# Batch 1's k.v as corner products, later exponentials and earlier output copies at the first seam of a fused attention and SwiGLU kernel

## The chip, the cores and the metric

One core of a Trainium2 chip. The metric is device microseconds of one execution. A run's time is about 1.8 us longer than the span that its profile shows (before: 310.9 against 309.1).

## The reference

Linear attention over 8 batches, 8 heads, 576 positions and head size 64, then a SwiGLU block over 4608 tokens:

```python
phi = lambda x: np.where(x > 0, x, np.exp(x) - 1.0) + 1.0
q_p, k_p = phi(q), phi(k)
kv  = np.einsum('bhsd,bhse->bhde', k_p, v)
z   = np.sum(k_p, axis=2)
num = np.einsum('bhsd,bhde->bhse', q_p, kv)
den = np.einsum('bhsd,bhd->bhs', q_p, z)[..., None] + 1e-06
x   = (num / den)            # brought to 4608 x 512
g   = x @ w_gate             # 512 x 1536
out = (g / (1 + np.exp(-g)) * (x @ w_val)) @ w_out
```

## The kernel before

The tokens go through in nine groups (0 to 8) of 512. For each group TensorE does a first product (twelve blocks of gate and value, `l1`) and a second product (`l2`, four output blocks for groups 0 and 1). The attention of later batches is woven between these blocks as lists of functions, one list for each block. On each engine the order of the program is the order of execution. The seam from group 0 to group 1 is the part that the change touches:

```python
    # batch 1's k.v: 64 rows by 128 columns, of which only two 64x64 corners are wanted
                    if b < 2:
                        nc.tensor.matmul(
                            out=kvb[b][hh][:, 256 * lp:256 * lp + P], lhsT=term_[rows, j, P * lp:P * lp + P],
                            rhs=v16[b][rows, 2 * lp:2 * lp + 2, D * j:D * j + D], ...)
                        continue
                    for e in range(2):                      # batch 2 and later: the corners alone
                        nc.tensor.matmul(
                            out=kvb[b][hh][D * e:D * e + D, 256 * lp:256 * lp + D + 1], ...)
    # ... cut ...
    def phi(src, e, dst, b, lp):          # batch 2: VectorE, min, then max and add fused
        s = slice(2 * lp, 2 * lp + 2)
        nc.vector.tensor_scalar(out=e[:, s, :], in0=e[:, s, :], scalar1=1.0, scalar2=None, op0=ALU.min)
        for l in range(2 * lp, 2 * lp + 2):
            nc.vector.scalar_tensor_tensor(out=dst[...], in0=src[...], scalar=0.0, in1=e[...], op0=ALU.max, op1=ALU.add)
    # ... cut ...
        w = at(12, [     # (after which of group 0's twelve output pieces, what)
            (0, lambda: t1(pX[0], 0, 4, A)), (1, lambda: t1(pX[1], 4, 7, V)), (1, lambda: z0(1, 0)),
            (1, lambda: z0(1, 1)), (1, lambda: z0_copy(1, 0)), (1, lambda: z0_copy(1, 1)),
            (2, lambda: t1(pX[0], 7, 9, A)), (2, lambda: mm1(1, 0)), (2, lambda: mm1(1, 1)), (2, lambda: r1_copies()),
            (3, lambda: den1(0)), (4, lambda: num1(0)), (4, lambda: exp_k(2, 0)), (5, lambda: den1(1)),
            (5, lambda: phi_k(2, 0)), (6, lambda: num1(1)), (6, lambda: exp_k(2, 1)), (7, lambda: den2()),
            (9, lambda: phi_k(2, 1)), (10, lambda: num2()), (10, lambda: exp_q(2, 0)), (11, lambda: exp_q(2, 1))])
    # ... cut ...
    for i in range(3):
        # ... cut ...
        for t in range(4):
            l2(0, t, 4 * i, 4 * i + 4)         # one piece: 4 matmuls of 128x512
            for f in w[4 * i + t]:
                f()
            if i == 2:
                l2_out(0, t, V)                # VectorE copies the bank out, SyncE stores it
```

`den1` and `num1` are products of 64x64 corners (denominators and numerators of batch 1; their operands `zz` and `R` are VectorE's copies of batch 1's k sums and k.v), `den2` and `num2` their tail of two columns of units; in the old `num2` VectorE's four tail products follow at once. A stretch of such 64x64 products between two 128-row blocks is called a visit below. `t1` is a transpose by TensorE, `mm1` is k.v, `exp_k`, `exp_q` and `l1_gate`'s silu run on ScalarE. `joint(2)` in group 1 needs batch 2's k sums and v copies; its `zd` and `R` copies lead to batch 2's normalising.

The last group's results leave in 16 store issues of 64 KB, 13 of them on SyncE's queue, two on ScalarE's and one on GpSimd's.

Of the kernel before, what the change touches and what calls it, by code (L numbers as in the profile page):

```python
# [13 lines left out]
P = 128  # L14
# [3 lines left out]
def kernel(  # L18
# [81 lines left out]
    def ld_k(b):  # L100
        load(k, k16, b)
# [11 lines left out]
    def ld_w2(i):  # L113
        nc.gpsimd.dma_start(out=wo[:, 4 * i:4 * i + 4, :],
                            in_=moe_w_out[512 * i:512 * i + 512, :].rearrange("(c p) f -> p c f", p=P))
# [3 lines left out]
        s = slice(2 * lp, 2 * lp + 2)  # L119
        nc.scalar.activation(out=e[:, s, :], in_=src[b % 2][:, s, :], func=AF.Exp, bias=0.0, scale=1.0)  # L120

    def phi(src, e, dst, b, lp):
        s = slice(2 * lp, 2 * lp + 2)
        nc.vector.tensor_scalar(out=e[:, s, :], in0=e[:, s, :], scalar1=1.0, scalar2=None, op0=ALU.min)
        for l in range(2 * lp, 2 * lp + 2):
            nc.vector.scalar_tensor_tensor(
                out=dst[b % 2][:, :, D * l:D * l + D],
                in0=src[b % 2][:, l, :].rearrange("p (j d) -> p j d", d=D), scalar=0.0,
                in1=e[:, l, :].rearrange("p (j d) -> p j d", d=D), op0=ALU.max, op1=ALU.add)

    def relu(src, dst, b, lp):
        s = slice(2 * lp, 2 * lp + 2)
        nc.scalar.activation(out=dst[b % 2][:, :, P * lp:P * lp + P].rearrange("p j (s d) -> p s j d", d=D),
# [9 lines left out]
    def phi_sum(e, dst, b, lp):  # L143
        s = slice(2 * lp, 2 * lp + 2)
        nc.vector.tensor_scalar(out=e[:, s, :], in0=e[:, s, :], scalar1=1.0, scalar2=None, op0=ALU.min)
        d = dst[b % 2][:, :, P * lp:P * lp + P].rearrange("p j (s d) -> p s j d", d=D)
        nc.vector.tensor_tensor(out=d, in0=d, in1=e[:, s, :].rearrange("p s (j d) -> p s j d", d=D), op=ALU.add)

    def exp_k(b, lp):
        exp_(k16, ek, b, lp)  # L150

    def exp_q(b, lp):
        exp_(q16, eq, b, lp)

    def phi_k(b, lp):
        phi_sum(ek, kp, b, lp) if b > 2 else phi(k16, ek, kp, b, lp)

    def phi_q(b, lp):
        phi_sum(eq, qp, b, lp) if b > 2 else phi(q16, eq, qp, b, lp)


    def vcast(b, lp):
# [12 lines left out]
    def mm1(b, lp):  # L175
        if lp == 0:
            kvb[b] = ((pV[2], pX[0]), (pX[2], pV[2]), (pX[0], pX[1]), (pV[0], pG[0]), (pX[2], pV[2]))[min(b, 4)]
        for j in range(J):
            for (t, term_) in enumerate(terms_k(b, lp)):
                for hh in range(2):  # L180
                    rows = slice(C * hh, C * hh + C)
                    if b < 2:
                        nc.tensor.matmul(
                            out=kvb[b][hh][:, 256 * lp:256 * lp + P], lhsT=term_[rows, j, P * lp:P * lp + P],
                            rhs=v16[b][rows, 2 * lp:2 * lp + 2, D * j:D * j + D],
                            start=(j == 0 and t == 0), stop=(j == J - 1 and t == len(terms_k(b, lp)) - 1))
                        continue
                    for e in range(2):
                        nc.tensor.matmul(  # L189
                            out=kvb[b][hh][D * e:D * e + D, 256 * lp:256 * lp + D + 1],  # L190
                            lhsT=term_[rows, j, P * lp + D * e:P * lp + D * e + D],
                            rhs=vm[b % 2][rows, j, 2 * lp + e, :], start=(j == 0), stop=(j == J - 1))

    def zdiag(b, lp):
        for hh in range(2):
# [9 lines left out]
                                 bias=0.0, scale=1.0)  # L205

    def kv(b):
        c1 = D if b < 2 else 0
        return lambda i, e: R[b % 2][D * e:D * e + D, i, c1 * e:c1 * e + D]

    def zs(i, e):
# [53 lines left out]
    def corners(ps, lhs, b, j0, j1, lps=(0, 1)):  # L265

        for lp in lps:
            for hh in range(2):
                for e in range(2):
                    rows = slice(D * e, D * e + D)  # L270
                    nc.tensor.matmul(out=ps[2 * lp + e][C * hh:C * hh + C, :], lhsT=lhs(2 * lp + hh, e),  # L271
                                     rhs=qT[b % 2][rows, j0:j1, lp, C * hh:C * hh + C], start=True, stop=True)
# [455 lines left out]
    ld_w2(0)  # L728
    ld_v(1)
    ld_w2(1)  # L730
    ld_k(2)
    ld_w2(2)


    def at(n, items):
        sl = [[] for _ in range(n)]
        for (i, f) in items:
            sl[i].append(f)
        return sl
# [8 lines left out]
    def t1(ps, j0, j1, eng):  # L748
        pt = ps[:, :].bitcast(FP16)
        for jj in range(j1 - j0):  # L750
            for lp in range(2):
                i = 2 * jj + lp
                nc.tensor.transpose(out=pt[:, P * i:P * i + P], in_=qp[1][:, j0 + jj, P * lp:P * lp + P],
                                    identity=id16[:, :])
        dst = qT[1][:, j0:j1, :, :].rearrange("p j l t -> p (j l t)")
        if eng == "A":
            nc.scalar.activation(out=dst, in_=pt[:, 0:2 * P * (j1 - j0)], func=AF.Copy, bias=0.0, scale=1.0)
        else:
            nc.vector.tensor_copy(out=dst, in_=pt[:, 0:2 * P * (j1 - j0)])
# [4 lines left out]
    def den1(lp):  # L764
        corners({2 * lp + e: dbank[e][:, 0:W7] for e in range(2)}, zs, 1, 0, 7, (lp,))
        ln0([b[:, 0:W7] for b in dbank], rr[:, 2 * lp:2 * lp + 2, 0:W7])
        exp_neg(rr[:, 2 * lp:2 * lp + 2, 0:W7])
# [12 lines left out]

    def num2():
        corners([nbank[m % 2][:, part1[m]] for m in range(4)], kv(1), 1, 7, 9)
        for m in range(4):
            x0(nbank[m % 2][:, part1[m]], r8[:, m % 2, part1[m]], xT[m][0][:, 0:W2])

    def r1_copies():
        for hh in range(2):
            nc.vector.tensor_copy(out=R[1][:, hh:4:2, 0:P],
                                  in_=kvb[1][hh][:, :].rearrange("p (i c) -> p i c", i=2)[:, :, 0:P])

    def block(src, e, dst):
        for lp in range(2):
            exp_(src, e, 1, lp)
            term(src[1], dst[1], lp, 0.0, ALU.max)
        for lp in range(2):
            phi_1(src, e, dst, lp)

    def first():
        sl = at(FB, [
            (3, lambda: block(k16, ek, kp)), (8, lambda: block(q16, eq, qp)),  # L800
            (11, lambda: nc.scalar.preload_act_table_set("natural_log_exp_and_others"))])
        w = at(12, [
            (0, lambda: t1(pX[0], 0, 4, A)), (1, lambda: t1(pX[1], 4, 7, V)), (1, lambda: z0(1, 0)),
            (1, lambda: z0(1, 1)), (1, lambda: z0_copy(1, 0)), (1, lambda: z0_copy(1, 1)),
            (2, lambda: t1(pX[0], 7, 9, A)), (2, lambda: mm1(1, 0)), (2, lambda: mm1(1, 1)), (2, lambda: r1_copies()),
            (3, lambda: den1(0)), (4, lambda: num1(0)), (4, lambda: exp_k(2, 0)), (5, lambda: den1(1)),
            (5, lambda: phi_k(2, 0)), (6, lambda: num1(1)), (6, lambda: exp_k(2, 1)), (7, lambda: den2()),
            (9, lambda: phi_k(2, 1)), (10, lambda: num2()), (10, lambda: exp_q(2, 0)), (11, lambda: exp_q(2, 1))])
        return sl, w

    def joint(b):
# [7 lines left out]
    def steady(b):  # L819

        n = 5 if b == 2 else 2 if b == 3 else 1
        items = [(n, lambda: zb(b)), (n, lambda: zb_copy(b)), (n, lambda: s3_prod(b, 0)),
                 (n + 1, lambda: s3_reduce(b, 0)), (n + 2, lambda: s3_recip(b, 0)), (n + 2, lambda: s3_prod(b, 1)),
                 (n + 3, lambda: s3_scale(b, 0)), (n + 4, lambda: s3_reduce(b, 1)), (n + 4, lambda: tr(b, 0)),
                 (n + 5, lambda: s3_recip(b, 1)), (n + 5, lambda: s3_prod(b, 2)), (n + 6, lambda: s3_scale(b, 1)),
                 (n + 7, lambda: s3_reduce(b, 2)), (n + 7, lambda: tr(b, 1)), (n + 8, lambda: s3_recip(b, 2)),
                 (n + 9, lambda: s3_scale(b, 2)), (n + 9, lambda: tr(b, 2))]
        if b == 2:
            items = [(0, lambda: vcast(2, 0)), (1, lambda: vcast(2, 1)), (1, lambda: phi_q(2, 0)),
                     (2, lambda: phi_q(2, 1)), (3, lambda: joint(2))] + items  # L830
        elif b == 3:
            items = [(0, lambda: phi_q(b, 1))] + items
        return at(FB, [x for x in items if x[0] < FB]), at(4, [(0, f) for (i, f) in items if i >= FB])
# [48 lines left out]
    for i in range(3):  # L882
        if i < 2:
            for m in range(4):
                w_sum(nc.gpsimd, m, 2 * i, 2 * i + 2)
        for t in range(4):
            l2(0, t, 4 * i, 4 * i + 4)
            for f in w[4 * i + t]:
                f()
            if i == 2:  # L890
                l2_out(0, t, V)
    nc.scalar.preload_act_table_set("silu_and_others")

    for g in range(1, NG):
# [87 lines left out]
```

## Time and profile before

| | before |
|---|---|
| time, median of 4 runs | 310.88 us (310.32 to 311.22) |
| span of the profiled run | 309.12 us |
| TensorE busy | 299.3 us, 97% |
| first group-0 output piece to group 1's third weight block | 18.56 us (38.83 to 57.39) |
| group 1's third weight block to its first output block | 20.17 us (57.39 to 77.56) |
| start of TensorE's last matmul to the end of the span | 6.28 us (302.84 to 309.12) |

The last two rows are differences of start times in the timeline; they leave out the run-to-run scatter of the start (the first group-0 output piece starts anywhere from 38.5 to 39.7 us; what sets it was not followed up).

The page, kernel before: the span, and busy us, share and instructions of each engine.

```profile
span 309.1 us, 6601 instructions
PE 299.3 (97%) x2551; PEld 183.0 (59%) x2551; DVE 252.0 (82%) x536; ACT 217.3 (70%) x336; POOL 48.2 (16%) x62
```

Timeline, kernel before, the seam (start us, duration us, engine, line, operation, out<-in; in brackets idle time before and what ended it):

```profile
53.32 1.43 DVE L126 SCALAR_TENSOR_TENSOR kp<-k,ek 128x576 f16<-128x576 f16 x2
53.72 1.04 PE L457 MATMUL pG<-wo,hT 128*128 128x512 f16 x4
54.66 0.68 DVE L467 TENSOR_SCALAR osb<-pG 128x512 f32<-128x512 f32 x1
...
55.40 1.02 PE L298 MATMUL pG<-xT,wg 128*128 128x512 f16 x4 [0.65 <-DVE osb L467]
...
56.06 0.68 DVE L467 TENSOR_SCALAR osb<-pV 128x512 f32<-128x512 f32 x1
56.26 1.03 PE L298 MATMUL pV<-xT,wv 128*128 128x512 f16 x4
56.66 0.68 DVE L467 TENSOR_SCALAR osb<-pG 128x512 f32<-128x512 f32 x1
57.39 1.02 PE L298 MATMUL pG<-xT,wg 128*128 128x512 f16 x4
```

Group 0's last output piece (53.72) is followed by group 1's first weight block only at 55.40, when VectorE has copied the bank `pG` out; VectorE was late because it did batch 2's k sum (53.32) first. The third weight block waits in the same way for the copy of 56.66.

Timeline of TensorE alone, kernel before, batch 1's k.v:

```profile
43.34 0.23 PE L183 MATMUL pX<-v,kp 64*128 64x128 f16 x1
...
44.45 1.04 PE L457 MATMUL pG<-wo,hT 128*128 128x512 f16 x4
45.41 0.38 PE L271 MATMUL pX<-qT,zz 64*64 64x448 f16 x4
45.73 1.04 PE L457 MATMUL pV<-wo,hT 128*128 128x512 f16 x4
46.70 0.37 PE L271 MATMUL pX<-qT,R 64*64 64x448 f16 x1
```

k.v takes 43.34 to 44.45, 1.11 us. The piece started at 44.45 has 0.86 us to stream (the distance of unbroken pieces).

Timeline, kernel before, group 1's ninth gate block:

```profile
69.64 1.03 PE L298 MATMUL pV<-xT,wv 128*128 128x512 f16 x4
70.01 0.60 ACT L303 ACTIVATE sil<-pG 128x512 f16<-128x512 f32 x1
70.66 1.02 PE L298 MATMUL pG<-xT,wg 128*128 128x512 f16 x4
```

The block of 70.66 could have started at 70.50 (69.64 + 0.86, the distance of unbroken blocks) and waits for the bank that the silu of 70.01 frees.

### The profile page before, as it was taken

The page shows a single profiled execution, that of the slowest core. Times are in us where ns is not written, and L with a number is a line of the kernel's source. Part 1 is how long each engine was busy: PE and PEld are TensorE (multiplying, and loading weights), DVE is VectorE, ACT ScalarE, POOL GpSimd, SP SyncE. Part 2 cuts the span into 40 slices and gives each one's busy share as a digit, 9 for nine tenths or more (in the row PEclk, how much of TensorE's full clock was granted, in tenths as well). Part 3 has the DMA queues.
Part 4 walks back from the last instruction along what each step waited for, and adds up shares of the span by engine and source line. Part 5 has one row for each costly group of instructions (what it writes and reads, how often), then busy time and mean ns, then how long its engine had stood idle before and what let it go on. Part 6 is the DMA issues. An engine that isn't in the chain of part 4 may idle for free.

```text
span 309.1 us, 6601 instructions
## 1 busy us (share of the span) xinstructions
PE 299.3 (97%) x2551; PEld 183.0 (59%) x2551; DVE 252.0 (82%) x536; ACT 217.3 (70%) x336; POOL 48.2 (16%) x62
## 2 busy tenths in 40 slices
PE   7899999999999999999999999999999999999992
PEld 6544453344444477447744774468446888878781
DVE  3757857888967998998899889997999878968971
ACT  3769969859856968696869686968633578448840
POOL 8535286010200002000200000000000004001200
PEclk9999999999999999999999999999999999999999
DMA  7999999998396228921793133122312140042013
GB/s 97 193 200 199 204 207 209 244 228 141 61 244 123 32 46 133 234 55 27 120 234 56 35 70 71 28 51 62 78 25 51 28 111 2 0 95 46 1 44 94
DMA packets 41424, 32.29 MB, mean 104 GB/s; under 512 B 16352, under 2 KB 37280, under 8 KB 41392
## 3 DMA queue, kind: packets, MB, share of 16 engines
q0 software_dynamic: 20672, 18.94, 39.1%
q1 hardware_dynamic: 20560, 12.79, 17.7%
q8 instruction: 20, 0.33, 0.4%
q10 hardware_dynamic: 160, 0.13, 0.2%
q14 instruction: 12, 0.10, 0.1%
HBM read 37.75 MB, written 9.44 MB: 153 GB/s over the span
## 4 chain that ended last, share of the span: by engine, by line
PE 84%; issue 5%; DMA 3%; DVE 3%; POOL 2%; ACT 1%; POOLq 0%
PE pV L298 22%; PE pG L298 22%; PE pX L513 14%; PE pV L513 4%; PE pV L350 4%; PE pG L350 4%; DMA wv<-in_moe_w_val_dram 3%; PE pX L298 3%; PE pG L457 2%; PE pV L457 2%; PE pX L350 1%; PE pV L271 1%; DVE xT L669 1%; PE pX L189 1%; PE pV L418 1%
## 5 line engine op out<-in xcount | busy, mean ns | idle before, releaser
L298 PE MATMUL pV<-xT,wv 128*128 128x512 f16 x324 | 83.5, 379 | 0.1
L298 PE MATMUL pG<-xT,wg 128*128 128x512 f16 x312 | 80.4, 379 | 0.8 <-DVE osb L467 0.6
L303 ACT ACTIVATE sil<-pG 128x512 f16<-128x512 f32 x78 | 45.9, 597 | 28.7 <-PE pG L298 18.0
L304 DVE SCALAR_TENSOR_TENSOR hT<-pV,sil 128x512 f16<-128x512 f32 x81 | 55.1, 687 | 13.0 <-ACT sil L303 6.8
L298 PEld LDWEIGHTS <-wv 128*128 128x128 f16 x336 | 32.7, 98 | 40.1 <-DMA wv<-in_moe_w_val_dram 0.9
L298 PEld LDWEIGHTS <-wg 128*128 128x128 f16 x336 | 32.2, 98 | 39.3 <-issue 1.8
L513 PEld LDWEIGHTS <-hs 128*128 128x128 f16 x336 | 32.4, 98 | 4.7 <-DVE hs L487 0.5
L390 POOL TENSOR_TENSOR hT<-prod,vm 128x512 f16<-128x512 f16 x6 | 6.9, 1156 | 132.0 <-ACT vm L377 132.0
L513 PEld LDWEIGHTS <-hT 128*128 128x128 f16 x252 | 24.3, 98 | 4.1
L513 PE MATMUL pX<-ws,hs 128*128 128x256 f16 x210 | 25.7, 273 | 0.0
L518 ACT ACTIVATE part<-pX 128x256 f32<-128x256 f32 x35 | 12.8, 381 | 13.2 <-PE pX L513 13.1
L95 POOL DMA_DIRECT2D k<-in_k_dram x7 | 5.2, 750 | 80.3 <-ACT part L518 58.8
L487 DVE TENSOR_TENSOR hs<-hT 128x512 f16<-128x512 f16 (+2 forms) x42 | 17.4, 418 | 0.2
L252 DVE TENSOR_TENSOR qp<-qp,rden 128x768 f16<-128x768 f16 x18 | 17.1, 949 | 0.0
L239 DVE TENSOR_REDUCE den<-prod 128x12 f32<-128x768 f16 x18 | 17.0, 943 | 0.0
L120 ACT ACTIVATE ek<-k 128x1152 f16<-128x1152 f16 x14 | 16.0, 1158 | 0.1
L120 ACT ACTIVATE eq<-q 128x1152 f16<-128x1152 f16 x14 | 15.6, 1167 | 0.0
L513 PE MATMUL pX<-wo,hT 128*128 128x256 f16 x126 | 15.2, 273 | 0.0
L457 PEld LDWEIGHTS <-hT 128*128 128x128 f16 x96 | 8.6, 98 | 10.2 <-issue 0.8
L164 ACT ACTIVATE vm<-v 128x1152 f16<-128x1152 f16 x12 | 14.1, 1178 | 0.0
L523 DVE SCALAR_TENSOR_TENSOR osb<-pX,part 128x256 f32<-128x256 f32 x28 | 10.7, 417 | 2.1 <-PE pX L513 1.9
L457 PE MATMUL pG<-wo,hT 128*128 128x512 f16 x48 | 11.7, 380 | 0.0
(185 smaller groups left out, 537.6 us busy)
## 6 DMA issues: line engine op xcount, KB each, us to landing
out_dram<-osb SPq DMA_DIRECT2D x64, 128.0 KB, 4.0
k<-in_k_dram POOLq DMA_DIRECT2D x7, 576.0 KB, 10.8
q<-in_q_dram POOLq DMA_DIRECT2D x7, 576.0 KB, 11.2
v<-in_v_dram POOLq DMA_DIRECT2D x7, 576.0 KB, 13.9
wg<-in_moe_w_gate_dram POOLq DMA_DIRECT2D x6, 256.0 KB, 11.6
wv<-in_moe_w_val_dram POOLq DMA_DIRECT2D x6, 256.0 KB, 12.0
wo<-in_moe_w_out_dram POOLq DMA_DIRECT2D x3, 512.0 KB, 15.8
out_dram<-osb SPq DMA_DIRECT2D x13, 64.0 KB, 2.0
```

The costliest lines, as they stand in the source:

```text
L120: nc.scalar.activation(out=e[:, s, :], in_=src[b % 2][:, s, :], func=AF.Exp, bias=0.0, scale=1.0)
L164: nc.scalar.activation(out=vm[b % 2][:, :, s, 0:D].rearrange("p j l d -> p l j d"), in_=v16[b % 2][:, s, :].rearrange("p l (j d) -> p l j ...
L239: nc.vector.tensor_reduce(out=den[:, HL * j0:HL * j1], in_=prod[:, 0:j1 - j0, :].rearrange("p j (l d) -> p (j l) d", d=D), axis=AX.X, op=A ...
L252: nc.vector.tensor_tensor(out=qv, in0=qv, in1=rden[:, HL * j0:HL * j1].unsqueeze(2).to_broadcast([P, HL * (j1 - j0), D]), op=ALU.mult)
L298: nc.tensor.matmul(out=ps[:, :], lhsT=src[:, i, P * fb:P * fb + P], rhs=xT[i][g % 2][:, :], start=(i == 0), stop=(i == 3))
L303: nc.scalar.activation(out=s[:, :], in_=pg[:, :], func=AF.Silu, bias=0.0, scale=1.0)
L304: nc.vector.scalar_tensor_tensor(out=hT[g % 2][:, fb, :], in0=pv[:, :], scalar=SC, in1=s[:, :], op0=ALU.mult, op1=ALU.mult)
L350: nc.tensor.matmul(out=dst[:, HN * e:HN * e + HN], lhsT=lhs, rhs=rhs, start=(n in (1, 2, 5) and e == 0 and c == 0), stop=(c == 1), skip_gr ...
L457: nc.tensor.matmul(out=pso[(g, t)][:, :], lhsT=hT[g % 2][:, fb, P * t:P * t + P], rhs=wo[:, fb, :], start=(fb == 0), stop=(fb == FB - 1))
L487: (eng or nc.vector).tensor_tensor(out=o, in0=a, in1=b, op=op)
L513: nc.tensor.matmul(out=(z if n in (2, 3, 5) else x)[:, 0:HD], lhsT=left(f), rhs=right(f), start=(f == 0 and n in (1, 2, 5)), stop=(f == HF ...
L518: nc.scalar.activation(out=part[:, 2 * i + tt, :], in_=(x if from_x else z)[:, 0:HD], func=AF.Copy, bias=0.0, scale=1.0 / SC)
```

## The change

Its intent: shorten batch 1's k.v by corner products, let TensorE pass the seam without waiting for VectorE's copies, start the denominators earlier by putting the ln table load behind the first transposed copy, take work off VectorE (a separate max and add in place of the fused form), and make sure the last third of `wo` is there in time.

```diff
-    def phi(src, e, dst, b, lp):        # ... the fused form, gone
     def phi_k(b, lp):
-        phi_sum(ek, kp, b, lp) if b > 2 else phi(k16, ek, kp, b, lp)
+        phi_sum(ek, kp, b, lp)
     # phi_q the same
@@ mm1
-                    if b < 2:
+                    if b == 0:
@@
+                        w = D if b == 1 else D + 1
                         nc.tensor.matmul(
-                            out=kvb[b][hh][D * e:D * e + D, 256 * lp:256 * lp + D + 1],
+                            out=kvb[b][hh][D * e:D * e + D, 256 * lp:256 * lp + w],
@@ loads
     ld_w2(1)
+    ld_w2(2)
     ld_k(2)
-    ld_w2(2)
@@ the lists at the seam
-        w = at(12, [ ... as above ... ])
+        w = at(13, [
+            (0, lambda: t1(pX[0], 0, 4, A)), (0, ln_set), (1, lambda: t1(pX[1], 4, 7, V)), (1, lambda: z0(1, 0)),
+            (1, lambda: z0(1, 1)), (1, lambda: z0_copy(1, 0)), (1, lambda: z0_copy(1, 1)),
+            (2, lambda: den1(0)), (2, lambda: mm1(1, 0)), (2, lambda: mm1(1, 1)), (2, lambda: r1_copies()),
+            (3, lambda: den1(1)), (3, lambda: num1(0)), (5, lambda: t1(pX[0], 7, 9, V)), (5, lambda: num1(1)),
+            (6, lambda: den2()), (6, lambda: exp_k(2, 0)), (6, lambda: exp_k(2, 1)), (7, lambda: max_2(k16, kp, 0)),
+            (7, lambda: max_2(k16, kp, 1)), (8, lambda: num2()), (9, lambda: phi_k(2, 0)), (9, lambda: exp_q(2, 0)),
+            (11, lambda: exp_q(2, 1)), (12, lambda: x2()), (12, lambda: phi_k(2, 1))])
@@ output copies
             l2(0, t, 4 * i, 4 * i + 4)
+            if (i, t) == (2, 1):
+                l2_out(0, 1, V)
             for f in w[4 * i + t]:
                 f()
-            if i == 2:
+            if i == 2 and t != 1:
                 l2_out(0, t, V)
+    for f in w[12]:
+        f()
```

(Cut: the kv and R indices that follow from the corners, `x2`, which is the second half of the old `num2`, and two `max_2` for q at the start of group 1.)

More of the change, by code (lines that the diff above doesn't have):

```diff
@@ L120, in exp_ @@
         nc.scalar.activation(out=e[:, s, :], in_=src[b % 2][:, s, :], func=AF.Exp, bias=0.0, scale=1.0)
-    def phi(src, e, dst, b, lp):
-        s = slice(2 * lp, 2 * lp + 2)
-        nc.vector.tensor_scalar(out=e[:, s, :], in0=e[:, s, :], scalar1=1.0, scalar2=None, op0=ALU.min)
-        for l in range(2 * lp, 2 * lp + 2):
-            nc.vector.scalar_tensor_tensor(
-                out=dst[b % 2][:, :, D * l:D * l + D],
-                in0=src[b % 2][:, l, :].rearrange("p (j d) -> p j d", d=D), scalar=0.0,
-                in1=e[:, l, :].rearrange("p (j d) -> p j d", d=D), op0=ALU.max, op1=ALU.add)
     def relu(src, dst, b, lp):
@@ L155, in phi_k @@
     def phi_k(b, lp):
-        phi_sum(ek, kp, b, lp) if b > 2 else phi(k16, ek, kp, b, lp)
+        phi_sum(ek, kp, b, lp)
     def phi_q(b, lp):
-        phi_sum(eq, qp, b, lp) if b > 2 else phi(q16, eq, qp, b, lp)
+        phi_sum(eq, qp, b, lp)
     def vcast(b, lp):
@@ L188, in mm1 @@
                     for e in range(2):
+                        w = D if b == 1 else D + 1
                         nc.tensor.matmul(
-                            out=kvb[b][hh][D * e:D * e + D, 256 * lp:256 * lp + D + 1],
+                            out=kvb[b][hh][D * e:D * e + D, 256 * lp:256 * lp + w],
                             lhsT=term_[rows, j, P * lp + D * e:P * lp + D * e + D],
-                            rhs=vm[b % 2][rows, j, 2 * lp + e, :], start=(j == 0), stop=(j == J - 1))
+                            rhs=v16[1][rows, 2 * lp + e, D * j:D * j + D] if b == 1 else vm[b % 2][rows, j, 2 * lp + e, :],
+                            start=(j == 0), stop=(j == J - 1))
     def zdiag(b, lp):
@@ L207, in kv @@
     def kv(b):
-        c1 = D if b < 2 else 0
+        c1 = D if b == 0 else 0
         return lambda i, e: R[b % 2][D * e:D * e + D, i, c1 * e:c1 * e + D]
@@ L782, in num2, with x2 @@
         corners([nbank[m % 2][:, part1[m]] for m in range(4)], kv(1), 1, 7, 9)
+    def x2():
         for m in range(4):
@@ L787, in r1_copies @@
         for hh in range(2):
-            nc.vector.tensor_copy(out=R[1][:, hh:4:2, 0:P],
-                                  in_=kvb[1][hh][:, :].rearrange("p (i c) -> p i c", i=2)[:, :, 0:P])
+            nc.vector.tensor_copy(out=R[1][:, hh:4:2, 0:D],
+                                  in_=kvb[1][hh][:, :].rearrange("p (i c) -> p i c", i=2)[:, :, 0:D])
     def block(src, e, dst):
@@ L796, in block, with max_2 @@
             phi_1(src, e, dst, lp)
+    def max_2(src, dst, lp):
+        term(src[0], dst[0], lp, 0.0, ALU.max)
     def first():
         sl = at(FB, [
-            (3, lambda: block(k16, ek, kp)), (8, lambda: block(q16, eq, qp)),
-            (11, lambda: nc.scalar.preload_act_table_set("natural_log_exp_and_others"))])
-        w = at(12, [
-            (0, lambda: t1(pX[0], 0, 4, A)), (1, lambda: t1(pX[1], 4, 7, V)), (1, lambda: z0(1, 0)),
+            (3, lambda: block(k16, ek, kp)), (8, lambda: block(q16, eq, qp))])
+        ln_set = lambda: nc.scalar.preload_act_table_set("natural_log_exp_and_others")
+        w = at(13, [
+            (0, lambda: t1(pX[0], 0, 4, A)), (0, ln_set), (1, lambda: t1(pX[1], 4, 7, V)), (1, lambda: z0(1, 0)),
             (1, lambda: z0(1, 1)), (1, lambda: z0_copy(1, 0)), (1, lambda: z0_copy(1, 1)),
-            (2, lambda: t1(pX[0], 7, 9, A)), (2, lambda: mm1(1, 0)), (2, lambda: mm1(1, 1)), (2, lambda: r1_copies()),
-            (3, lambda: den1(0)), (4, lambda: num1(0)), (4, lambda: exp_k(2, 0)), (5, lambda: den1(1)),
-            (5, lambda: phi_k(2, 0)), (6, lambda: num1(1)), (6, lambda: exp_k(2, 1)), (7, lambda: den2()),
-            (9, lambda: phi_k(2, 1)), (10, lambda: num2()), (10, lambda: exp_q(2, 0)), (11, lambda: exp_q(2, 1))])
+            (2, lambda: den1(0)), (2, lambda: mm1(1, 0)), (2, lambda: mm1(1, 1)), (2, lambda: r1_copies()),
[3 more added lines that the diff above has]
+            (11, lambda: exp_q(2, 1)), (12, lambda: x2()), (12, lambda: phi_k(2, 1))])
         return sl, w
@@ L828, in steady @@
         if b == 2:
-            items = [(0, lambda: vcast(2, 0)), (1, lambda: vcast(2, 1)), (1, lambda: phi_q(2, 0)),
-                     (2, lambda: phi_q(2, 1)), (3, lambda: joint(2))] + items
+            items = [(0, lambda: vcast(2, 0)), (1, lambda: vcast(2, 1)), (1, lambda: max_2(q16, qp, 0)), (1, lambda: phi_q(2, 0)),
+                     (2, lambda: max_2(q16, qp, 1)), (2, lambda: phi_q(2, 1)), (3, lambda: joint(2))] + items
         elif b == 3:
```

## The prediction

> **What bounds the kernel now.** TensorE. The page's busy table gives PE 299.3 of 309.1 us (97%) at full granted clock; the chain of waits is 84% PE. In the stretch the change touches (39 to 78 us) the timeline shows three places where PE idles or works avoidably:
>
> 1. Group 0's last output block starts at 53.72 and takes 0.86, yet group 1's first weight block starts at 55.40 (waits: PE pG on DVE osb, 0.65) and its third at 57.39 instead of 57.13. VectorE, in order, does batch 2's k sum and batch 1's tail products before the output copies (0.68 each, ending 55.34 and 57.34) that free the banks. Lost: about 0.8 + 0.25 = 1.05 us.
> 2. Batch 1's k.v: 36 matmuls 64x128, 43.34 to 44.45 = 1.11 us. Batch 2's, as 64x64 corners, takes 0.74 (72 matmuls, 85.78 to 86.52). The Trainium skill, "TensorEngine Tiling (Array Packing)", Available Configurations, gives four 64x64 tiles against two 64x128; the trace agrees in direction, 0.74 against 1.11.
> 3. At 70.66 PE waits 0.16 for silu (ACT, ending 70.61).
>
> **What the change does.**
> - Corners: -0.37 us of PE, on the path. R copies shrink, off it.
> - Output copies before the tail products and second k sum: banks free near 53.0 and 55.5, against PE's new arrivals near 54.05 and 55.78: -1.05 us, on the path.
> - The ln table load (1.28 us in the trace; "ScalarE: Activation LUTs", What ACT_TABLE_LOAD costs, says about 1283 ns) moves behind the first qT copy, which starts near 40.65, not 41.94. Denominators start a block earlier.
> - phi of batch 2: max 0.41 + min 0.49 + add 0.67 instead of 0.49 + 1.34 on VectorE: -0.26 us a half; two q halves fall in group 1.
> - The four exps run after the tail's exp, about 50.9 to 55.3, against an end at 55.61 before.
> - wo third 2 landed 49.9 for a first use at 50.78, which would come near 50.3: insurance, no gain. It lands near 47, k2 near 49.9 instead of 47.4, ahead of its exp.
>
> **How much is kept.** PE alone would be 1.4 to 1.6 us earlier at group 1. But there the others chain: silu after the table load, VectorE's q sums, zd, ScalarE's R copies (idle 3.19 on zd), then a dense ScalarE run to 78 that PE meets at 70.66 with no slack. In order: silu of block 1 comes about 0.6 earlier, the q sums save 0.52, so zd and silu 4 to 6 come about 1.15 earlier. PE should wait 0.3 to 0.5 us more at group 1's blocks 6 to 8. Later groups are PE-bound and pass the rest on. Kept: about 1.2 us.
>
> **Predicted: 309.8 us, 309.0 to 310.7 (8 in 10).** Faster by over 2%: 0.01; within 2%: 0.98; slower by over 2%: 0.01.
>
> **What would show it.** Timeline: first group-1 weight block near 54.05 with no wait on osb, third near 55.8; batch 1's k.v about 0.74 us; first denominator corners near 43.0. In group 1 PE waits for ACT's silu before block 6, 7 or 8, and the one that started at 70.66 starts near 69.5; its end at 77.56 becomes about 76.4. From there all marks lie 1.1 to 1.3 us earlier to the end. Wrong on the loss: no such wait and the shift stays 1.5.
>
> **What would make it wrong.** k2 landing after 50.9, holding exps and so silu 0 (PE waits at group 1's third block); output copies late because the k sum waits for its exp (up to 0.5 less); denominators waiting for zz or qT at 43.0; ScalarE's dense run holding PE more (gain 0.7) or less (1.6).

## More of the kernel before

TensorE is the bound, and the trace has 2551 matmuls of it and as many weight loads.

## The result, and the profile after

| | before | after |
|---|---|---|
| time, median of 4 runs | 310.88 us | 308.30 us (307.90 to 308.66) |
| ratio | | 0.9918, 95% interval 0.9896 to 0.9941 |
| span of the profiled run | 309.12 | 306.12 |
| first output piece to third weight block | 18.56 | 16.60 (38.81 to 55.42) |
| third weight block to group 1's first output block | 20.17 | 20.32 (55.42 to 75.74) |
| TensorE's last matmul to the end of the span | 6.28 | 5.14 (300.99 to 306.12) |

A ratio is the mean time of one kernel's runs over that of the other's of the same rounds, so it is not quite the ratio of the medians quoted here. The gain is 2.6 us where 1.2 was predicted, and the time lies below the stated range.

Between the end of group 1 and TensorE's last matmul the two kernels agree within 0.03 us. So the 2.99 us between the two profiled spans are: 1.96 won at the seam, 0.15 given back in group 1, and 1.14 won after TensorE has finished; the 0.04 left over are the start and the groups between.

The page, kernel after:

```profile
span 306.1 us, 6673 instructions
PE 298.9 (98%) x2587; PEld 183.2 (60%) x2587; DVE 251.7 (82%) x537; ACT 216.7 (71%) x335; POOL 48.7 (16%) x62
```

There are 36 more matmuls and 36 more weight loads, 72 more TensorE instructions, from the corner form.

Timeline, kernel after, the seam:

```profile
52.16 0.69 DVE L460 TENSOR_SCALAR osb<-pG 128x512 f32<-128x512 f32 x1 [0.51 <-PE pG L450]
...
52.83 1.03 PE L450 MATMUL pG<-wo,hT 128*128 128x512 f16 x4
...
53.69 1.03 PE L291 MATMUL pG<-xT,wg 128*128 128x512 f16 x4
...
54.53 0.68 DVE L460 TENSOR_SCALAR osb<-pG 128x512 f32<-128x512 f32 x1
54.55 1.03 PE L291 MATMUL pV<-xT,wv 128*128 128x512 f16 x4
...
55.42 1.03 PE L291 MATMUL pG<-xT,wg 128*128 128x512 f16 x4
```

The copy of `pG` is done before TensorE comes, and 52.83, 53.69, 54.55 and 55.42 follow at 0.86 to 0.87 us: no wait is left at the seam.

Timeline of TensorE alone, kernel after, k.v and the visits:

```profile
43.02 0.38 PE L264 MATMUL pX<-qT,zz 64*64 64x448 f16 x4
43.23 0.19 PE L181 MATMUL pX<-v,kp 64*64 64x64 f16 x1
...
43.97 1.04 PE L450 MATMUL pG<-wo,hT 128*128 128x512 f16 x4
44.94 0.38 PE L264 MATMUL pX<-qT,zz 64*64 64x448 f16 x4
45.15 0.35 PE L264 MATMUL pX<-qT,R 64*64 64x448 f16 x1
...
45.44 1.04 PE L450 MATMUL pV<-wo,hT 128*128 128x512 f16 x4
```

k.v takes 43.23 to 43.97, 0.74 us, as forecast. What was not forecast: denominators and numerators now stand in one visit, and the way from 43.97 to 45.44 is 0.86 + 0.61 us. Before, the visit of `zz` corners lengthens the way from 44.45 to 45.73 by 0.42 us: two visits of 0.42 have become one of 0.61. In the same way `den1(0)` now shares a visit with k.v.

Timeline, kernel after, group 1's ninth gate block:

```profile
67.67 1.03 PE L291 MATMUL pV<-xT,wv 128*128 128x512 f16 x4
68.19 0.60 ACT L296 ACTIVATE sil<-pG 128x512 f16<-128x512 f32 x1
68.83 1.02 PE L291 MATMUL pG<-xT,wg 128*128 128x512 f16 x4
```

The wait for silu is there, and it is 0.30 us (67.67 + 0.86 = 68.53) against 0.16 before.

The rest is in the tail. Timeline of SyncE's queue and of VectorE, kernel before, first two store issues, each alone, then the last two issues together, then the last result:

```profile
300.08 1.55 SPq L530 DMA_DIRECT2D out_dram<-osb  x1
...
303.00 0.76 SPq L530 DMA_DIRECT2D out_dram<-osb  x1
...
305.13 1.18 SPq L530 DMA_DIRECT2D out_dram<-osb  x2
...
303.15 0.42 DVE L539 TENSOR_SCALAR osb<-pX 128x256 f32<-128x256 f32 x1 [0.31 <-PE pX L513]
```

The transfer queues of the same kernel between 299.9 and 301.3 us (packets, MB, share of the 16 engines):

```profile
q8 instruction: 1, 0.02, 5.5%
```

The same issue, the last issue and the last result, kernel after:

```profile
298.23 0.59 SPq L523 DMA_DIRECT2D out_dram<-osb  x1
...
302.75 0.55 SPq L523 DMA_DIRECT2D out_dram<-osb  x1
...
301.30 0.42 DVE L532 TENSOR_SCALAR osb<-pX 128x256 f32<-128x256 f32 x1 [0.31 <-PE pX L506]
```

And its queues between 293.9 and 295.3 us; between 298.0 and 299.4 there is no such packet:

```profile
q8 instruction: 1, 0.02, 4.7%
```

The last results are ready at 303.57 before and 301.72 after, 1.85 us apart, which is the gain of the body. But SyncE's last issue starts at 305.77 (the second of the two in the line of 305.13) and at 302.75, 3.02 us apart. SyncE issues at a distance of 0.60 to 0.68 us without a gap at the end (once 0.81, behind the issue of 303.00), so whatever stops the queue once is still there at the end. In the kernel before one issue, at 300.08, takes 1.55 us where its twin after takes 0.59, and the one at 303.00 takes 0.76 where its twin takes 0.55: 0.96 and 0.21 us, which are the 1.17 by which 3.02 exceeds 1.85. And at 300.02 an instruction fetch of 16,384 bytes begins on queue 8. After, that fetch begins at 294.01. The Trainium skill, "Runtime: NRT & Kernel Launch", Instruction fetch mechanics, says that an engine's instructions are refilled in blocks of 16 KiB, 256 instructions each. For TensorE this agrees: queue 8 has 20 packets of that size for some 5,100 TensorE instructions. The page calls the cost of crossing a block "mostly hidden".

### The profile page after: what moved, and what is told of

The parts are those of the page before. It is cut to its first block, busy times and chain, and to the rows that moved or that the text cites. A ratio compares the mean times of both kernels' runs of the same rounds, so it can differ in the third digit from the quotient of the medians. Undisturbed runs are those within 1.5% of the kernel's fastest.

```text
span 306.1 us, 6673 instructions
## 1 busy us (share of the span) xinstructions
PE 298.9 (98%) x2587; PEld 183.2 (60%) x2587; DVE 251.7 (82%) x537; ACT 216.7 (71%) x335; POOL 48.7 (16%) x62
## 4 chain that ended last, share of the span: by engine, by line
PE 80%; DMA 10%; issue 5%; ACT 2%; POOL 1%; POOLq 0%; ACTq 0%
PE pG L291 20%; PE pV L291 20%; PE pX L506 14%; DMA wg<-in_moe_w_gate_dram 4%; DMA wv<-in_moe_w_val_dram 4%; PE pV L506 4%; PE pV L343 4%; PE pG L343 4%; PE pG L450 4%; PE pV L450 3%; DMA k<-in_k_dram 2%; PE pX L343 1%; PE pV L264 1%; PE pX L181 1%; PE pV L411 1%
```

## The experiments

Theory: the body's gain is as the prediction laid it out (C in the texts below), with a mis-sized sum, the visits (M); and 1.14 us of the gain comes from the tail, because 72 more TensorE instructions move TensorE's last instruction fetch out of the time of SyncE's last issues (T). Rivals: the tail is scatter (R); the gain at the seam comes from the load order or the exps rather than from the copies; group 1's VectorE work is free. What the ln table load's move and batch 2's k halves in the new form are worth alone was not tested.

Every kernel below was correct. "Seam", "group 1" and "tail" are the three stretches of the tables above, from each run's own profile, one for each kernel. The experiments ran in three batches (t, b, c), each with its own runs of the kernel before (medians 310.96, 310.60 and 310.95 us; the pair of before and after had 310.88), so that times of different batches compare better by their ratios.

| kernel | time, us | ratio to before (95%) | seam | group 1 | tail | longest late issue |
|---|---|---|---|---|---|---|
| before | 310.88 | | 18.56 | 20.17 | 6.28 | 1.55 |
| after | 308.30 | 0.9918 (0.9896 to 0.9941) | 16.60 | 20.32 | 5.14 | 0.59 |
| t1_before_split | 310.44 | 0.9981 (0.9963 to 0.9999) | 18.41 | 20.17 | 5.10 | 0.59 |
| t2_after_split92 | 309.43 | 0.9944 (0.9926 to 0.9962) | 16.60 | 20.33 | 6.26 | 1.45 |
| t3_after_nocorner | 309.72 | 0.9954 (0.9936 to 0.9971) | 17.07 | 20.33 | 6.27 | 1.72 |
| t4_after_nocorner_split | 308.90 | 0.9931 (0.9912 to 0.9949) | 17.12 | 20.33 | 5.11 | 0.59 |
| b1_after_unmerge | 308.71 | 0.9940 (0.9923 to 0.9956) | 16.83 | 20.33 | 5.10 | 0.59 |
| b2_after_oldphi_q | 308.69 | 0.9943 (0.9928 to 0.9958) | 16.61 | 21.09 | 5.11 | 0.59 |
| b3_after_oldout | 309.46 | 0.9964 (0.9949 to 0.9979) | 17.96 | 20.02 | 5.10 | 0.59 |
| b4_after_k2first | 308.02 | 0.9929 (0.9910 to 0.9949) | 16.65 | 20.33 | 5.13 | 0.59 |
| c1_before_corners | 309.47 | 0.9957 (0.9944 to 0.9969) | 18.17 | 20.17 | 5.10 | 0.59 |
| c2_before_tail | 309.12 | 0.9940 (0.9927 to 0.9954) | 18.48 | 20.18 | 4.68 | 1.56 |
| c3_after_tail | 307.17 | 0.9878 (0.9863 to 0.9893) | 16.61 | 20.33 | 4.01 | 0.59 |
| c4_after_best | 306.68 | 0.9866 (0.9852 to 0.9879) | 16.65 | 20.04 | 4.01 | 0.59 |

### t1_before_split: the kernel before, with more TensorE instructions

```diff
     def l1_mm(g, fb, w, i):
+        if g == 2 and fb < 5:
+            for h in range(2):
+                cs = slice(256 * h, 256 * h + 256)
+                nc.tensor.matmul(out=ps[:, cs], lhsT=..., rhs=xT[i][g % 2][:, cs],
+                                 start=(i == 0 and h == 0), stop=(i == 3), skip_group_check=True)
+            return
```

> The kernel before, with 40 of group 2's 512-column matmuls cut into two of 256 columns: the same columns streamed, 80 more TensorE instruction rows (5104 to 5184), nothing else touched. Theory T (tail): the kernel before loses about 1.1 us at its end because TensorE's 16 KB instruction fetch (the trace has it at 300.0) falls onto SyncE's last output issues, one of which took 1.55 us instead of 0.59; the new kernel's fetch came at 294.0 only because its TensorE stream is 72 rows longer. T expects the fetch about 8 us before TensorE's end instead of 3, no output issue over 0.8 us, last TensorE work within 0.2 us of before, and the time about 1.0 us less: 309.9 against 310.9, ratio 0.997. Rival R (the tail has nothing to do with the instruction count; the 1.2 us is run-to-run scatter): same time within 0.3 us, ratio 1.000.

The fetch came at 294.17, the late issue took its usual time, and the tail went from 6.28 to 5.10. Timeline of SyncE's queue in this run, the issue that corresponds to that of 300.08:

```profile
300.66 0.59 SPq L536 DMA_DIRECT2D out_dram<-osb  x1
```

The time fell by 0.5 us and not by the 1.0 expected, though the interval of the ratio, 0.9963 to 0.9999, holds both that and almost nothing: in the profiled run the first group-0 output piece started at 39.47 instead of 38.83, and TensorE's last matmul 0.58 later. The 40 cuts account for 0.10 of the difference (group 2's first product took 21.03 us instead of 20.93), the rest is the scatter of the start. The median of six runs carries that scatter too, so the tail's own number is the better reading. The tail follows the instruction count here and in the next three runs; rival "scatter" falls on the four together.

### t2_after_split92: the kernel after, with one more fetch

The same edit, for 92 matmuls of group 2 (`fb < 11 or w == 0`).

> The new kernel with 92 matmuls of group 2 cut in two (5176 to 5360 rows), so that one more instruction fetch comes, about 3 us before TensorE's end, where the kernel before has its own. T: an output issue of about 1.5 us appears in the tail and the time goes back up by 1.0 to 1.3 us (0.2 of it for the cuts themselves): about 309.5, ratio to before 0.9955. R: only the 0.2 us of the cuts, about 308.5, ratio 0.992.

21 fetches now, the last at 298.87. The tail is 6.26 again and the time up by 1.1 us against the kernel after (0.8 by the ratios). SyncE's queue:

```profile
298.91 1.45 SPq L529 DMA_DIRECT2D out_dram<-osb  x1
```

A matmul-splitting edit in group 2, some 200 us earlier, makes the end longer. T holds in both directions.

### t3_after_nocorner and t4_after_nocorner_split

t3 restores `if b < 2:` and its indices; t4 adds the edit of t1.

> The new kernel with batch 1's k.v put back to 36 matmuls of 64x128 (5104 rows again, the same as before). By the corner reckoning of the prediction TensorE is 0.37 us later from group 1 on. T: besides, the fetch returns to about 3 us before TensorE's end and the tail is 1.1 us longer: about 309.7, ratio 0.996. R: only 0.37: about 308.7, ratio 0.993.

> As the last one, with 40 matmuls of group 2 cut in two (5184 rows). T: the fetch leaves the tail again, what remains is the corners' own 0.37 us and 0.1 for the cuts: about 308.8, ratio 0.9935, some 0.9 us less than the run without the cuts. R: no better than that run, 0.1 us worse.

t3: the tail is back at 6.27, and the fetch (299.04) is next to an issue of 1.72 us:

```profile
299.06 1.72 SPq L523 DMA_DIRECT2D out_dram<-osb  x1
```

t4: tail 5.11, 0.82 us faster than t3 by the medians of the same batch, though it has 40 cuts more. The seam is 17.07 and 17.12, so that the corners are worth 0.47 to 0.52 us of TensorE. The prediction had 0.37, from k.v alone (1.11 - 0.74, which the traces of before and after confirm). Part of the remaining 0.1 goes with `den1(0)`, which shares k.v's visit here: the way between the blocks around k.v grows by 0.47 from after to t3 (1.92 to 2.39), and shrinks by 0.42 from before to c1 (2.32 to 1.90), where `den1(0)` stands elsewhere. The rest is open.

### b1_after_unmerge: one visit more

```diff
-            (3, lambda: den1(1)), (3, lambda: num1(0)), (5, ...
+            (3, lambda: num1(0)), (4, lambda: den1(1)), (5, ...
```

> The new kernel with the second denominators' corners taken out of the visit they share with the first numerators and given one of their own, a block later (as in the kernel before). Theory M (visits): a stretch of 64x64 corner products between 128-row blocks costs TensorE about 0.23 us beyond the streaming, whatever its length (a lone one took 0.42, two together 0.61), and the change merged two pairs, which the prediction did not count. M expects the stretch from the first group-0 output block to group 1's third weight block to go from 16.61 to about 16.84 us, time about 308.5. Rival (the prediction's reckoning, where only the corners' own 0.37 and the bank waits count): that stretch stays at 16.6.

Seam 16.83, just the 0.23 expected. The time rose by 0.4 us (0.7 by the ratios); the profiled run's start was 0.87 later than that of the kernel after, so the seam is again the better reading. The Trainium skill, "TensorEngine Tiling (Array Packing)", Key Properties, says that changing the tiling mode drains TensorE; it names no price. This case's price is 0.23 us for a visit of 64x64 products between 128-row blocks; that it is the drain is the page's word, which no run here separates from the visit's other costs. The change takes two such visits away.

### b2_after_oldphi_q: the q sums in the old form

```diff
     def phi_q(b, lp):
-        phi_sum(eq, qp, b, lp)
+        phi_sum(eq, qp, b, lp) if b > 2 else phi(q16, eq, qp, b, lp)
     # and without the two max_2(q16, qp, ...)
```

> The new kernel with batch 2's q sums put back to the fused form on VectorE (0.49 + 1.34 us a half, no separate max). Theory C (the prediction's chain): the q sums stand on the chain VectorE q sums, zd, ScalarE's R copies and its dense run, which TensorE meets at group 1's ninth gate block; the new kernel waits 0.3 us there. C expects zd and that run about 0.6 us later, that wait 0.9 us, and the stretch from group 1's third weight block to its first output block to go from 20.32 to about 20.9, time about 308.9. Rival (group 1 has slack, the sums are free): 20.3 and 308.3.

Group 1 takes 21.09 instead of 20.32, 0.77 us more (0.6 expected). Timeline of this run at the seventh and the ninth gate block:

```profile
65.43 1.02 PE L300 MATMUL pG<-xT,wg 128*128 128x512 f16 x4 [0.28 <-ACT sil L305]
...
68.76 0.60 ACT L305 ACTIVATE sil<-pG 128x512 f16<-128x512 f32 x1
...
69.40 1.02 PE L300 MATMUL pG<-xT,wg 128*128 128x512 f16 x4 [0.36 <-ACT sil L305]
```

Both waits are for silu, as theory C has it, but only one stands where it was expected. The ninth block loses 0.53 us (0.9 expected; 0.30 in the kernel after), 0.23 more; the other 0.53 is lost at the seventh, where the kernel after does not wait at all. So the size came out right with the place half wrong. VectorE's saving of 0.3 us a half, off the bottleneck by any view of busy shares, is worth 0.77 us of TensorE.

### b3_after_oldout: the old order of the output copies

```diff
-            if (i, t) == (2, 1):
-                l2_out(0, 1, V)
...
-            if i == 2 and t != 1:
+            if i == 2:
...
-            (11, lambda: exp_q(2, 1)), (12, lambda: x2()), (12, lambda: phi_k(2, 1))])
+            (9, lambda: x2()), (10, lambda: phi_k(2, 1)), (11, lambda: exp_q(2, 1))])
```

> The new kernel with the old order on VectorE at the end of group 0: tail products and both k sums before output copies 1, 2 and 3. By the prediction's reckoning of the bank waits TensorE should wait about 0.65 us at group 1's first block and again about 0.65 at its third: the stretch from the first group-0 output block to group 1's third weight block goes from 16.61 to about 17.9. Of this 0.3 is given back at the ninth gate block, where the wait for silu vanishes (20.32 to about 20.0), so the time is about 1.0 us up, 309.3. Rival (the exps moved later had already taken the copies off the path): less than 0.3 us.

Seam 17.96 (17.9 expected), group 1 20.02 (20.0). Timeline:

```profile
54.91 1.02 PE L291 MATMUL pG<-xT,wg 128*128 128x512 f16 x4 [0.56 <-DVE osb L460]
...
57.27 0.59 PE L291 MATMUL pG<-xT,wg 128*128 128x512 f16 x2 [0.47 <-DVE osb L460]
```

Both bank waits return. The early copies are the largest single piece of the seam, 1.36 us here, of which 0.3 is given back at the ninth gate block. (It is more than the 1.08 that the kernel before lost, as TensorE now arrives earlier and both k sums stand late; the pieces of the seam are not to be added up from such runs.)

### b4_after_k2first: the old load order

```diff
-    ld_w2(2)
     ld_k(2)
+    ld_w2(2)
```

> The new kernel with batch 2's k loaded ahead of the last third of the output weights, as before. The weights should land near 49.9 instead of 47, and their first user now comes at 49.89 (before: 50.78). Theory I (insurance): no more than 0.3 us lost at that block, often nothing, time 308.3 to 308.6. Rival (the load order carries part of the gain): 0.5 us or more lost there.

All three stretches are the same within 0.05 us. The weights landed at 49.2 (issued 30.47, 18.7 us to landing) for a first use at 49.65. The order is insurance, as the prediction said.

### c1_before_corners: the corners alone

The hunk of `mm1` and its indices, put into the kernel before.

> The kernel before with nothing but the corner form of batch 1's k.v (5176 TensorE rows instead of 5104). By the runs so far the corners are worth 0.49 us of TensorE (stretch from the first group-0 output block to group 1's third weight block 18.56 to about 18.07, unless VectorE's late copies, which stay where they were, take it back: then 18.5), and the longer stream moves the last instruction fetch out of the tail (end of TensorE to end of the span 6.28 to about 5.1). Theory T: time down by 1.2 to 1.6 us, 309.4, most of it from the tail. By the prediction's reckoning, which had no tail term: down by 0.4 at most, 310.5.

The time falls by 1.5 us. Of this 1.18 is the tail, 0.39 the seam (0.42 won at k.v; the bank wait for `osb` stays, and the way that it lengthens grows from 1.69 to 1.77). Against t1 and c2, whose seams are 18.41 and 18.48, the 0.39 would be 0.24 to 0.31. So an edit whose own worth is 0.4 to 0.5 us shows three times that.

### c2_before_tail and c3_after_tail: two issues given to GpSimd

```diff
+        dg = [lambda: put(g, 0, 0, HD, DM, (nc.sync, nc.gpsimd)), lambda: put(g, 0, 1, 0, HD, (nc.sync, nc.gpsimd))]
-                ... (p[4][0], c12[0], d[0][0][1]), (p[5][1], c21[0], d[0][1][0]), ...
+                ... (p[4][0], c12[0], dg[0]), (p[5][1], c21[0], dg[1]), ...
```

> The kernel before with one output issue of two late pairs given from SyncE's queue to GpSimd's. T says the stalled issue costs time because eight issues of about 0.64 us each stand behind it without a gap. With two fewer there is room: the stall itself may stay (about 1.5 us), but the end of TensorE to the end of the span falls from 6.28 to about 4.5 and the time by 1.5 us or more, to about 309.3. If the fetch slowed the transfers themselves rather than the queue, the end would stay over 5.5.

> The new kernel with the same two issues given to GpSimd. SyncE's last issue comes at 301.8 instead of 302.75, right behind the last result; end of TensorE to end of the span 5.13 to about 4.2, time about 307.4. If the landing of the last transfer and not the queue sets the end: 5.1 and 308.3.

SyncE's slow issue in c2, and its last issue in c3:

```profile
300.00 1.56 SPq L530 DMA_DIRECT2D out_dram<-osb  x1
```

```profile
302.25 0.47 SPq L523 DMA_DIRECT2D out_dram<-osb  x1
```

In c2 the slow issue is still there, but the tail falls to 4.68: the fetch costs time through the queue behind it, not through the transfers. Two issues fewer do not make room for all of it: the last one starts at 304.44, 0.95 us after the last result, and the tail is 0.67 longer than in c3. In c3 SyncE's last issue comes at 302.25, when its result is ready, and the tail is 4.01, so the queue of issues set the end in the kernel after as well. The Trainium skill, "DMA: Bandwidth & Descriptors", Issuing engines are not separate DMA queues, says that issuing from several engines saves only the sequencer's issue time, "which is usually small relative to the DMA itself". Here that time was the critical path: 1.13 us of tail for two issues.

### c4_after_best: c3, and group 1's later ScalarE work one block later

```diff
-                sl[4 + lp].append(lambda lp=lp: relu_k(b2, lp))
-                sl[6 + lp].append(lambda lp=lp: relu_q(b2, lp))
-                sl[8 + lp].append(lambda lp=lp: vcast(b2, lp))
+                d = 1 if g == 1 else 0
+                sl[4 + lp + d * lp].append(lambda lp=lp: relu_k(b2, lp))
+                sl[6 + lp + d].append(lambda lp=lp: relu_q(b2, lp))
+                sl[8 + lp + d].append(lambda lp=lp: vcast(b2, lp))
```

> The last one, and in group 1 ScalarE's second relu of batch 3's k, its two relus of q and its two v copies moved one block later, so that the silu which TensorE waits 0.3 us for at the ninth gate block comes 1.15 us earlier. By theory C the stretch from group 1's third weight block to its first output block goes from 20.32 to about 20.0, with no wait for silu, and the time to about 307.1. If ScalarE's dense run only passes the wait on to a later block: 20.3 and 307.4.

The ninth gate block in this run is that of 68.66, 0.86 us after the block before it:

```profile
67.80 1.03 PE L291 MATMUL pV<-xT,wv 128*128 128x512 f16 x4
...
68.66 1.03 PE L291 MATMUL pG<-xT,wg 128*128 128x512 f16 x4
```

Group 1 takes 20.04: the wait for silu is gone and does not come back at a later block. 306.68 us is the fastest of all, 1.6 us under the kernel after by the medians. Its gain over c3 (ratios 0.9866 and 0.9878) lies inside the two intervals; the stretch of 20.04 against 20.33 is what shows it.

## Why the prediction was wrong

Point by point:

- **Bound, and the three places of loss: right.** The bank waits vanished as described, and b3 brings them back, at the two blocks named.
- **"-1.05 us, on the path": right.** In the traces the two waits of before (0.82 and 0.26, as differences of block starts) are gone.
- **Corners, "-0.37 us of PE": undersized.** k.v went to 0.74 us as said, but taking the corners away costs 0.47 to 0.52 (t3, t4).
- **"PE alone would be 1.4 to 1.6 us earlier at group 1": undersized.** It was 1.97 (57.39 to 55.42). The missing term is the visits: the reordering puts `den1(0)` into k.v's visit and `den1(1)` into `num1(0)`'s. The second merging is worth 0.23 us (b1); the first was not undone alone, but the sum needs it: what the ways between blocks hold beyond the 0.86 of a block came to 3.14 us for k.v and the four visits after it before, and to 2.30 for the same work after, 0.84 less, against 0.37 + 2 x 0.23 = 0.83. Of the 0.42 us of a lone visit, more than half is thus the price of the visit and not of its products.
- **"zd and silu 4 to 6 come about 1.15 earlier": undersized.** The R copies came 1.82 earlier (65.69 to 63.87). The chain is the one named, with one link missing. Its start came earlier than said: TensorE's tail denominators, which the saved visits also moved, let the exps begin at 50.54 and not at 50.9, and silu of block 1 came 0.77 and not 0.6 earlier. But before, VectorE's product of block 1, behind which the q sums stand, had waited for TensorE's `pV` and not for silu, so that it moved with the seam, by 1.05 (59.38 to 58.33). The q sums saved 0.61, not 0.52, and `zd` came 1.66 earlier (64.85 to 63.19). So TensorE lost 0.15 more in group 1 and not 0.3 to 0.5, at the ninth block, where the block named began at 68.83 and not at 69.5.
- **"Kept: about 1.2 us": 1.8.** TensorE's last matmul starts 1.85 us earlier.
- **"From there all marks lie 1.1 to 1.3 us earlier to the end": this is the step that failed.** It takes for granted that the end of the program follows TensorE's end at a fixed distance. The distance was 6.28 us before and 5.14 after, in every profile one of these two values as long as the issues stayed where they were, and which of the two depends on where TensorE's instruction fetch falls (t1 to t4). With the body's 1.85 alone the time would have been about 309.0 (310.88 - 1.85), at the very edge of the range; with the body's predicted 1.2 and the tail's 1.14 it would have been about 308.5, outside it. So the tail is the step that counts, and the body's mis-sized sum the lesser one. The sign of a warning was in the profile of before: one issue of 1.55 us among issues of 0.6, with the queue full behind it. What put the fetch elsewhere was the count of the corners' instructions, a side effect that the prediction did not count and the change was not meant to have: the tail's 1.1 us is luck.
- **"insurance, no gain": right** (b4).

By the medians the gain is 2.58 us, by the two profiled spans 2.99; the kernel after has two runs near 307.9 and two near 308.6, and what divides them is not settled. The runs do not show either by what path a fetch by TensorE holds an issue of SyncE up for about a microsecond; that it does rests on four profiles where the fetch and the slow issue begin within 0.06 us of each other (300.02 and 300.08, 298.87 and 298.91, 299.04 and 299.06, 300.00 and 300.00), and on eight kernels with the issues unmoved and the fetch earlier, at 292.5 to 295.9, that have none (after, t1, t4, b1 to b4 and c1). The packet times in the fourteen traces carry it further. Of SyncE's 1072 store issues 54 took over 0.70 us; 28 of these overlap a fetch of queue 8, most of them far from the tail, and each of the 28 ends 0.37 or 0.38 us after that fetch's packet (before: 300.08 + 1.55 = 301.63 against 300.02 + 1.23 = 301.25; 122.38 + 1.30 = 123.68 against 122.35 + 0.96 = 123.31). So the slow issue ends with the fetch. Overlap alone is not enough (after: the issue of 116.50 lies inside a fetch of 115.99 to 117.19 and took 0.47), and the other 26, of up to 1.10 us, the one at 303.00 among them, overlap no fetch of queue 8; their cause is open.

## What to carry to other kernels

Read the tail, from the bounding engine's last instruction to the end of the span, as a stage of its own before predicting: a queue of issues without gaps there hands every stall on to the end, and a small edit far away can move one in or out. Cost a short stretch of work in another tiling mode by the visit and not by its streaming alone, and look for visits that can be merged. When the time of an edit and the work it removed differ by a factor of three, undo the side effect (here the instruction count) before believing either.

## What the Trainium skill lacked or had wrong

- "Runtime: NRT & Kernel Launch", Instruction fetch mechanics: it calls the cost of crossing a 16 KiB block mostly hidden. TensorE's last fetch, when it fell onto SyncE's late store issues, made one of them 1.45 to 1.72 us instead of 0.59 and, with the queue full behind it, the tail 1.12 to 1.18 us longer. No page names the effect of one engine's fetch on another's DMA issues.
- "CRC Debugging", Comparing the Two Runs, puts the instruction refills on queue 14. The 16,384-byte fetches that follow TensorE's instruction count (20 for 5,102 instructions, 21 for 5,358) are on queue 8; queue 14 carries others, of 8,192 bytes.
- "TensorEngine Tiling (Array Packing)": no price for a change of tiling mode. Here the difference was 0.23 us for each visit of 64x64 products between 128-row blocks.
- "DMA: Bandwidth & Descriptors", Issuing engines are not separate DMA queues: no case in which the time of issuing bounds a program. Here an undisturbed 64 KB store took 0.47 to 0.59 us of SyncE's queue and the issues followed at 0.60 to 0.68 us, which bounded the tail: two issues moved to GpSimd were worth 1.13 us.
- "ScalarE: Activation LUTs", What ACT_TABLE_LOAD costs: 1283 ns and a drain of 1380 ns, 2.66 us in all. The load took 1.28 us here, but ScalarE's exp ended at 54.84, the load ran from 54.86 to 56.14 and the next silu began at 56.16 (kernel after), 1.32 us in all.
